# Cosformer attention and a low-rank mixer on one core: tokens dealt five and four to the two halves of the partitions, and another order for batch 0

## The chip, the cores and the metric

The kernel runs on one core of one Trainium2 chip. The metric is device time in microseconds for one execution, lower is better. Each version is timed in several executions; one more is taken by the hardware profiler, and its trace is what the tables and lines here come from.

## The reference, cut to what matters

There are 8 batches of 576 tokens, 8 heads of 64 columns, all in float32. Attention is linear: q and k go through a ReLU and are weighted with a cosine and a sine of the token's position, and softmax is replaced by a division by a sum.

```python
theta = np.pi / 2.0 * pos / S
def phi(x, c, s):
    r = np.maximum(x, 0.0)
    return np.concatenate([r * c, r * s], axis=-1)
kv  = einsum('bhsf,bhsd->bhfd', phi(k), v)          # 128 x 64 for each head
num = einsum('bhsf,bhfd->bhsd', phi(q), kv)
den = einsum('bhsf,bhf->bhs', phi(q), sum_s phi(k)) + 1e-6
x   = num / den                                     # 576 x 512 for each batch
u   = x + (x.T @ U @ V).T                           # mixing of tokens, rank 32
out = u + relu(u @ w_ch1) @ w_ch2                   # 512 -> 2048 -> 512
```

The weights are U (576 x 32), V (32 x 576), w_ch1 (512 x 2048) and w_ch2 (2048 x 512).

## The kernel before, in words

**Tokens on partitions.** 576 tokens are four and a half times 128. Batch b's first 512 tokens are loaded so that partition p holds tokens 4p to 4p+3 (`load_main`, L74): 128 partitions, 8 heads, rows of 1024 bytes. Column group c (0 to 3) of a staging tile is then a tile of 128 tokens. The last 64 tokens form the tail, c = 4, in a tile of its own (`load_tail`, L80: rows of 256 bytes), in the lower 64 partitions for even batches and the upper 64 for odd ones (`tail`, L49), so that two batches' tails fill one tile of 128 tokens. Everything that works with tokens follows this layout: the position weights (iota, L117 and L122), the loads of U (L134, L138), the order of V's columns (`spread_v`, L191) and the stores (L556 for the tails, L560 for the rest: token group c is 128 rows of 2048 bytes, four tokens apart).

**The steps for one batch.** q and k are multiplied on VectorE and ScalarE (`prep`, L228 and L226), v is cast (`v_prep`, `v_block`, L103 and L105). `kv_unit` (L260) gives kv and the denominators' vector for four heads. q is transposed, in batches 0 and 1 on TensorE (`qtr_unit`, L277), later by DMA (`qtr_dma`, L290 and L295). Then come x (`x_unit`, or `den_unit`, L319, and `xh_unit`, L336 and L340, in batch 0), A = x.T U (`A_unit`, L379 and L385), and u = x + V A, both as it is (`u_unit`, L399 and L402) and transposed (`uTd_open`, L438, and `uTd_mm`, L452, in batches 0 and 1; by DMA after that, L422 and L428). The two large products are `g1_main` and `g1_tail` (L487, L507; ScalarE applies the ReLU, L496) and `g2_part` (L540), which adds u on VectorE (L550) and stores.

**What sets the order.** The schedule is written out by hand: each engine runs its instructions in program order. Batches go in pairs; a list of slots has the pair's large products (first batch's g1, second's g1, the tails' g1, then nine blocks of g2), and a table PLAN puts the attention of later batches between them. The head of the program, up to the first g1, has only batch 0's chain: `chain_head`, `chain_mid` and `chain_end` (L645 to L685). It takes four heads at a time; the first four heads' kv, denominators and x run before v of the other four has been cast. It is filled with matmuls on zeros (`keep_warm`, L171: 18, 2 and 13 of them, and seven in `warm0`), whose results nobody reads.

**Queues.** Loads and DMA transposes are issued by SyncE (SP); w_ch1 (`w1_load`, L91) and w_ch2 (`w2_load`, L97) are issued by GpSimd (POOL), which casts them on the way to bf16. The last pair's stores go through SP, the very last part through ScalarE, all others through POOL. POOL's queue in the head: a copy of one column of k's tail (`mark`, L703), which holds back what follows till that has landed, w1's first two quarters, the casts of U and V (`cast_uv`), w1's other two, and a second mark on k of batch 1 (L719), behind which w2 is issued. U and V themselves are the last of SP's loads for batch 0.

**Buffers.** PSUM has eight banks: tags g (3), o (2), T (1) and X (one of two banks). The stores' tile o_sb has four buffers. Each staging tile has one.

Of the kernel before, what the change touches and what calls it, by code (L numbers as in the profile page):

```python
# [13 lines left out]
ALU = mybir.AluOpType  # L14
# [3 lines left out]
def kernel(  # L18
# [29 lines left out]

    def tail(b):  # L49
        lo = TS * (b % 2)  # L50
        return slice(lo, lo + TS)
# [8 lines left out]
    kst, vst, qst, kt, vt, qt = {}, {}, {}, {}, {}, {}  # L60

    def alloc_k(b):
        kst[b] = pool.tile([P, H, 4, D], FP32, tag="kst", bufs=1, name="kst")
        kt[b] = pool.tile([P, H, D], FP32, tag="kt", bufs=1, name="kt")

    def alloc_v(b):
        vst[b] = pool.tile([P, H, 4, D], FP32, tag="vst", bufs=1, name="vst")
        vt[b] = pool.tile([P, H, D], FP32, tag="vt", bufs=1, name="vt")

    def alloc_q(b):  # L70
        qst[b] = pool.tile([P, H, 4, D], FP32, tag="qst", bufs=1, name="qst")
        qt[b] = pool.tile([P, H, D], FP32, tag="qt", bufs=1, name="qt")

    def load_main(dst, src, b, h0=0, h1=H, eng=None):  # L74
        (eng or nc.sync).dma_start(  # L75
            out=dst[:, h0:h1, :, :].rearrange("p h c d -> p h (c d)"),
            in_=src[b, h0:h1, 0:512, :].rearrange("h (p c) d -> p h (c d)", c=4),
        )

    def load_tail(dst, src, b, eng=None):  # L80
        (eng or nc.sync).dma_start(  # L81
            out=dst[tail(b), :, :],
            in_=src[b, :, 512:S, :].rearrange("h s d -> s h d"),
        )
# [16 lines left out]
    def cast(eng, o, i):  # L101
# [10 lines left out]

    alloc_k(0)
    alloc_q(0)
    alloc_v(0)
    iota = const.tile([P, 5], FP32)
    nc.gpsimd.iota(  # L117
        out=iota[:, 0:4], pattern=[[1, 4]], base=0, channel_multiplier=4,
        allow_small_or_imprecise_dtypes=True,
    )  # L120
    for lo in (0, TS):
        nc.gpsimd.iota(  # L122
            out=iota[lo : lo + TS, 4:5], pattern=[[1, 1]], base=512, channel_multiplier=1,
            allow_small_or_imprecise_dtypes=True,
        )
    load_main(qst[0], q, 0)
    load_tail(qt[0], q, 0)
    load_main(kst[0], k, 0)
    load_tail(kt[0], k, 0)
    load_tail(vt[0], v, 0)  # L130
    load_main(vst[0], v, 0, 0, 4)
    load_main(vst[0], v, 0, 4, 8)
    nc.sync.dma_start(out=stV, in_=moe_V)
    nc.sync.dma_start(  # L134
        out=stU[:, 0:4, :], in_=moe_U[0:512, :].rearrange("(p c) r -> p c r", c=4)
    )
    for lo in (0, TS):
        nc.sync.dma_start(out=stU[lo : lo + TS, 4, :], in_=moe_U[512:S, :])  # L138
# [7 lines left out]
    nc.scalar.activation(out=sinw, in_=iota, func=AF.Sin, bias=0.0, scale=scale_ang)  # L146
    nc.scalar.activation(out=cosw, in_=iota, func=AF.Sin, bias=halfpi, scale=-scale_ang)
# [14 lines left out]
    for i in range(2):  # L162
        V_.memset(v_ext[i][:, 4, :, :], 0.0)
        V_.memset(v_ext[i][:, 0:4, :, D:E], 1.0)
        V_.memset(v_ext[i][tail(i), 4, :, D:E], 1.0)
# [10 lines left out]
    V_.memset(U_bf, 0.0)  # L176
    mark = const.tile([TS, 1], FP32)
# [7 lines left out]
    def cast_uv():  # L185
        cast(G_, V_nat, stV)
        cast(G_, U_bf[:, 0:4, :], stU[:, 0:4, :])
        for i in range(2):
            cast(G_, U_bf[tail(i), 4 + i, :], stU[tail(i), 4, :])

    def spread_v(eng):  # L191
# [7 lines left out]
        cast(eng, V_bf, v_ps[:, 0, :].rearrange("r (p c) -> r c p", c=4))  # L199
# [6 lines left out]
    def v_prep(b, h0=0, h1=H, cs=range(5), engs=None):  # L206
        vx = v_ext[b % 2]
        for n, c in enumerate(cs):
            eng = engs[n] if engs else G_
            if eng is None:  # L210
                continue
            if c < 4:
                cast(eng, vx[:, c, h0:h1, 0:D], vst[b][:, h0:h1, c, :])
            else:
                cast(eng, vx[tail(b), 4, h0:h1, 0:D], vt[b][tail(b), h0:h1, :])

    def v_block(b, h0, h1, c0, c1, eng):
# [3 lines left out]
            vst[b][:, h0:h1, c0:c1, :],  # L221
# [10 lines left out]
    def prep(dst, src, b, c, engs, h0, h1):  # L232
        rows = slice(0, P) if c < 4 else tail(b)
# [6 lines left out]
    def k_prep(b, c, engs, h0=0, h1=H):  # L240
        if b not in k_p:
            k_p[b] = pool.tile([P, 4, H, 2 * D], BF16, tag="k_p", bufs=1, name="k_p")
        src = kst[b][:, h0:h1, c, :] if c < 4 else kt[b][:, h0:h1, :]
        prep(k_p[b][:, c] if c < 4 else k_tl, src, b, c, engs, h0, h1)

    def q_prep(b, c, engs, h0=0, h1=H):
        if b not in q_p:
            q_p[b] = pool.tile([P, 4, H, 2 * D], BF16, tag="q_p", bufs=1, name="q_p")
        src = qst[b][:, h0:h1, c, :] if c < 4 else qt[b][:, h0:h1, :]
# [23 lines left out]
    def qtr_unit(b, c, h0=0, h1=H, eng=None, tag="T", bufs=1):  # L273
# [10 lines left out]
        else:  # L284
            cast(eng or V_, q_tlT[:, h0:h1, tail(b)], t_ps[:, h0:h1, tail(b)])

    def qtr_dma(b, c0, c1):
# [6 lines left out]
        else:  # L294
            nc.sync.dma_start_transpose(  # L295
                out=q_tlT[:, :, tail(b)],
                in_=q_tl[tail(b), :, :].rearrange("p h f -> p (h f)"),
# [223 lines left out]
    def g2_part(pr, cc, part):  # L521
# [32 lines left out]
        if cc == 4:  # L554
            for i in range(2):
                eng.dma_start(  # L556
                    out=out[2 * pr + i, 512:S, :], in_=o_sb[i * TS : i * TS + TS, :]
                )
        else:
            eng.dma_start(  # L560
                out=out[b, 0:512, cols].rearrange("(p c) n -> p c n", c=4)[:, c, :],
# [4 lines left out]
    def loads(b, eng):  # L566
        def kk():
            alloc_k(b)
            load_tail(kt[b], k, b, eng)
            load_main(kst[b], k, b, eng=eng)  # L570

        def vv():
            alloc_v(b)
            load_tail(vt[b], v, b, eng)
            load_main(vst[b], v, b, eng=eng)

        def qq():
            alloc_q(b)
            load_tail(qt[b], q, b, eng)
            load_main(qst[b], q, b, eng=eng)  # L580

        return qq, kk, vv
# [21 lines left out]
    def attention_plan(b):  # L604
# [32 lines left out]
        for at, t in zip(lo, loads(b + 1, nc.sync) if lo else ()):  # L637
# [7 lines left out]
    def chain_head(b, fill, xt, engs):  # L645
        v_prep(b, 0, 4, (4,), (engs[0],))
        v_block(b, 0, 4, 0, 3, V_)
        v_block(b, 0, 4, 3, 4, engs[0])
        kv_unit(b, 0, "T", 1)
        fill(0)  # L650
        rec0 = den_unit(b, 0, 4, "X", 1)
        v_prep(b, 4, 8, (4,), (A_,))
        v_block(b, 4, 8, 0, 4, A_)
        fill(1)
        for n, c in enumerate(ORD):
            xh_unit(b, c, 0, 4, rec0, *xt[n])
            if n == 1:
                fill(2)
            if n == 3:
                kv_unit(b, 1, "T", 1, A_)  # L660

    def chain_mid(b, fill, xt, dt):
        fill(3)
        m = 3
        rec1 = den_unit(b, 4, 8, *dt)
        for n, c in enumerate(ORD[:m]):
            xh_unit(b, c, 4, 8, rec1, *xt[n])
        u01 = ps.tile([P, 2, 512], FP32, tag="X", bufs=1, name="u01")
        uTd_open(b, 0, None, None, u01[:, 0, :].rearrange("p (c t) -> p c t", c=4))
        uTd_open(b, 1, None, None, u01[:, 1, :].rearrange("p (c t) -> p c t", c=4))  # L670
        a0 = A_unit(b, "T", 1, A_, 0, 256)
        fill(4)
        uTd_mm(b, 0)
        uTd_mm(b, 1)
        uTd_evac(b, 0, A_)
        uTd_evac(b, 1, A_)
        for n, c in enumerate(ORD[m:]):
            xh_unit(b, c, 4, 8, rec1, *xt[m + n])
        fill(5)
        return a0  # L680

    def chain_end(b, a0):
        A_unit(b, "T", 1, V_, 256, 512, a0)
        uTd_open(b, 2, "o", 2)
        uTd_open(b, 3, "o", 2)  # L685

    def warm0(n):
        m = (2, 1, 0, 1, 1, 2)[n]
        if m:
            keep_warm(m, *(O2 if n == 0 else G3))  # L690

    keep_warm(18, "X", 1)
# [142 lines left out]
```

## Time and profile before

| what | us |
|---|---|
| median of 3 runs | 313.55 (313.11 to 314.17) |
| the profiled execution, its device time | 313.45 |
| its span, first to last instruction | 311.7 |
| TensorE busy with matmuls | 303.7 (97%) |
| VectorE, ScalarE, GpSimd busy | 153.4, 137.5, 46.2 |
| first g1 matmul (L487) starts | 22.98 |
| first g2 matmul (L540) starts, after a wait of 1.04 for w_ch2 | 41.75 |
| last store issued | 308.65 |
| DMA moved | 53.21 MB in 88987 packets, 171 GB/s |

The span is counted from the first instruction; all times of a line are in it. Between the span and the device time lie 1.8 us in which nothing of the program runs. PE is TensorE (PEld its weight loads), DVE VectorE, ACT ScalarE, POOL GpSimd, SP SyncE. L540 is line 540 of the kernel before. In a line of the timeline the first number is the start, the second the duration, both in microseconds, `x4` says that four equal instructions are merged into the line, and the bracket behind has the idle time of the engine ahead of it and what ended that. `DMA_DIRECT2D` is the issue of a transfer, not the transfer; q behind an engine's name is its sequencer.

### The profile page before, as it was taken

To read this page: it belongs to the slowest core of one execution; us is meant where nothing else is said; L and a number is where in the kernel's file an instruction comes from. 1 tells how busy PE (TensorE), PEld (TensorE's weight loads), DVE (VectorE), ACT (ScalarE), POOL (GpSimd) and SP (SyncE) were. 2 spreads that over 40 slices of the span, in tenths; PEclk is the share of its full clock that TensorE was granted. 3 is DMA by queue.
4 is the path that set the end of the run, shared out by engine and by line. 5 is a ranking of instruction groups with operands and counts; after the bars stand their busy time and mean duration, and the time that the engine had idled before them with its cause. 6 is when DMAs were issued, how large, how long until landed. Compare 5 with 4: busy or idle time off the path is not lost.

```text
span 311.7 us, 5648 instructions
## 1 busy us (share of the span) xinstructions
PE 303.7 (97%) x2314; PEld 157.6 (51%) x2314; DVE 153.4 (49%) x340; ACT 137.5 (44%) x229; POOL 46.2 (15%) x85
## 2 busy tenths in 40 slices
PE   7899989999999999999999999999999999999995
PEld 2566445445654444574455444484455444474443
DVE  5868835695878575046426584046426520002111
ACT  3846640265740366669400366669400366640000
POOL 2230300250031007003321400002320100000000
PEclk9999999999999999999999999999999999999999
DMA  7999999989996989992899589922871150001131
GB/s 215 281 244 228 254 183 257 325 200 247 273 178 131 265 200 208 234 306 60 187 226 306 209 103 211 304 76 53 180 157 69 67 86 0 0 2 67 67 103 67
DMA packets 88987, 53.21 MB, mean 171 GB/s; under 512 B 57122, under 2 KB 86178, under 8 KB 88962
## 3 DMA queue, kind: packets, MB, share of 16 engines
q1 hardware_dynamic: 82386, 41.52, 57.2%
q0 software_dynamic: 6432, 11.27, 15.1%
q8 instruction: 18, 0.29, 0.4%
q10 hardware_dynamic: 144, 0.07, 0.1%
q14 instruction: 7, 0.06, 0.0%
HBM read 36.86 MB, written 9.44 MB: 149 GB/s over the span
## 4 chain that ended last, share of the span: by engine, by line
PE 86%; issue 6%; DMA 4%; SPq 2%; POOL 1%; DVE 0%; POOLq 0%
PE o_ps L540 40%; PE g_ps L487 31%; PE gt_ps L507 5%; PE kv_ps L260 3%; PE x_ps L354 3%; DMA vst<-in_v_dram 2%; PE va_ps L399 2%; DMA w_bf<-in_moe_w_ch_dram 2%; SPq L81 1%; PE a_ps L379 1%; POOL w_bf L91 0%; PE va_ps L402 0%; SPq L75 0%; POOL U_bf L105 0%; PE d_ps L319 0%
## 5 line engine op out<-in xcount | busy, mean ns | idle before, releaser
L496 ACT ACTIVATE hid<-g_ps 128x512 bf16<-128x512 f32 x128 | 76.2, 597 | 105.5 <-PE g_ps L487 105.5
L540 PE MATMUL o_ps<-w_bf,hid 128*128 128x512 bf16 (+2 forms) x528 | 120.0, 372 | 1.0 <-DMA w_bf<-in_moe_w_ch_dram 1.0
L487 PE MATMUL g_ps<-uT,w_bf 128*128 128x512 bf16 x512 | 117.8, 379 | 0.1
L487 PEld LDWEIGHTS <-w_bf 128*128 128x128 bf16 x512 | 48.8, 98 | 58.0 <-issue 2.0
L540 PEld LDWEIGHTS <-hid 128*128 128x128 bf16 x528 | 48.2, 98 | 52.0 <-DMA w_bf<-in_moe_w_ch_dram 1.5
L550 DVE TENSOR_TENSOR o_sb<-u_bf,o_ps 128x512 f32<-128x512 bf16 (+2 forms) x33 | 22.0, 668 | 56.3 <-PE o_ps L540 56.2
L560 POOL DMA_DIRECT2D out_dram<-o_sb x24 | 13.2, 550 | 129.5 <-DVE o_sb L550 67.7
L406 DVE TENSOR_TENSOR u_bf<-x_bf,va_ps 128x512 bf16<-128x512 bf16 x32 | 21.9, 686 | 10.4 <-PE va_ps L399 10.4
L105 DVE CAST kv<-kv_ps 128x260 bf16<-128x260 f32 x15 | 6.4, 429 | 38.1 <-PE kv_ps L260 38.1
L364 DVE TENSOR_TENSOR x_bf<-x_ps,rec 128x512 bf16<-128x512 f32 x28 | 19.4, 691 | 1.0
L311 DVE TENSOR_SCALAR rec<-x_ps 128x8 f32<-128x8 f32 (+1 forms) x35 | 5.8, 165 | 22.8 <-PE x_ps L354 22.3
L507 PE MATMUL gt_ps<-uT_tl,w_bf 128*128 128x128 bf16 x256 | 15.9, 219 | 0.0
L507 PEld LDWEIGHTS <-w_bf 128*128 128x128 bf16 x256 | 14.7, 98 | 0.9
L540 PE MATMUL o_ps<-w_bf,hid_tl 128*128 128x512 bf16 x64 | 14.8, 379 | 0.0
L105 POOL CAST v_ext<-vst 128x512 bf16<-128x512 f32 x22 | 13.7, 653 | 3.6 <-DMA vst<-in_v_dram 3.4
L354 PEld LDWEIGHTS <-q_pT 128*128 128x128 bf16 x224 | 10.7, 98 | 6.4 <-DVE x_bf L364 0.4
L174 PE MATMUL w_ps<-zero 128*128 128x512 bf16 x40 | 11.6, 422 | 1.8 <-DVE halfpi L142 1.2
L226 ACT ACTIVATE k_p<-kst,sinw 128x512 bf16<-128x512 f32 x19 | 13.3, 708 | 0.0
L260 PEld LDWEIGHTS <-k_p 128*128 128x128 bf16 x256 | 11.2, 97 | 3.9 <-ACT v_ext L103 0.7
L228 DVE TENSOR_SCALAR q_p<-qst,cosw 128x512 bf16<-128x512 f32 x24 | 12.0, 513 | 2.1 <-DMA qst<-in_q_dram 2.0
L514 ACT ACTIVATE hid_tl<-gt_ps 128x512 bf16<-128x512 f32 x16 | 9.6, 597 | 6.6 <-PE gt_ps L507 6.6
L260 PE MATMUL kv_ps<-v_ext,k_p 128*128 128x65 bf16 x256 | 11.8, 193 | 0.4 <-DVE v_ext L105 0.4
(104 smaller groups left out, 234.2 us busy)
## 6 DMA issues: line engine op xcount, KB each, us to landing
qst<-in_q_dram SPq DMA_DIRECT2D x8, 1024.0 KB, 7.6
kst<-in_k_dram SPq DMA_DIRECT2D x8, 1024.0 KB, 10.3
vst<-in_v_dram SPq DMA_DIRECT2D x7, 1024.0 KB, 10.0
out_dram<-o_sb POOLq DMA_DIRECT2D x24, 256.0 KB, 3.7
w_bf<-in_moe_w_ch_dram POOLq DMA_DIRECT2D x8, 512.0 KB, 11.6
out_dram<-o_sb SPq DMA_DIRECT2D x7, 256.0 KB, 2.3
qt<-in_q_dram SPq DMA_DIRECT2D x8, 128.0 KB, 4.2
kt<-in_k_dram SPq DMA_DIRECT2D x8, 128.0 KB, 7.8
```

What stands on the lines that cost most here:

```text
L105: eng.tensor_copy(out=o, in_=i)
L226: nc.scalar.activation(out=o, in_=i, func=AF.Relu, bias=0.0, scale=w)
L260: nc.tensor.matmul(out=acc[:, i, :], lhsT=k_p[b][:, c, h, :] if c < 4 else k_tl[:, h, :], rhs=vx[:, c, h, :], start=(c == 0), stop=(c == 4),)
L354: nc.tensor.matmul(out=acc[:, g, i * E : i * E + E], lhsT=qT_of(b, c, h), rhs=kv_sb[b][:, h, :], start=True, stop=True,)
L364: nc.vector.tensor_tensor(out=x_of(b, c, rows).rearrange("p (g i d) -> p g i d", g=2, d=D), in0=view[:, :, :, 0:D], in1=rec[rows].unsqueez ...
L406: nc.vector.tensor_tensor(out=u_bf[b][:, c, :] if c < 4 else u_tl[b // 2], in0=x_of(b, c), in1=va, op=ALU.add,)
L487: nc.tensor.matmul(out=g_ps.rearrange("p (c t) -> p c t", c=4), lhsT=w1_bf[:, d, j * P : j * P + P], rhs=uT[b][:, :, d, :], start=(d == 0) ...
L496: nc.scalar.activation(out=hid[b][:, j, :], in_=g_ps, func=AF.Relu, bias=0.0, scale=1.0)
L507: nc.tensor.matmul(out=g_ps[:, jj, :], lhsT=w1_bf[:, d, j * P : j * P + P], rhs=uT_tl[pr][:, d, :], start=(d == 0), stop=(d == 3),)
L540: nc.tensor.matmul(out=o[:, cols], lhsT=lhs[:, j, c * P : c * P + P], rhs=w2_bf[:, j, cols], start=(j == 0), stop=(j == NJ - 1),)
L550: nc.vector.tensor_tensor(out=o_sb[:, cols], in0=u[:, cols], in1=o[:, cols], op=ALU.add)
L560: eng.dma_start(out=out[b, 0:512, cols].rearrange("(p c) n -> p c n", c=4)[:, c, :], in_=o_sb[:, cols],)
```

## The change

Token m*9+k goes to another place. Of each nine tokens in a row, the first five go to partition m (of 0 to 63) and the other four to partition 64 + m. There are no tail loads: a tensor's load is one transfer to the lower 64 partitions (rows of 1280 bytes) and one to the upper 64 (1024). Column group c (0 to 3) then holds tokens 9m+c and 9m+5+c; c = 4, which is the tail, holds tokens 9m+4, in the lower half, for every batch. The transposes put an odd batch's tail into the upper half of the shared tile, as before.

```diff
-            in_=src[b, h0:h1, 0:512, :].rearrange("h (p c) d -> p h (c d)", c=4),
...
-            in_=src[b, :, 512:S, :].rearrange("h s d -> s h d"),
...
+    def load(dst, src, b, h0=0, h1=H, engs=(nc.sync, nc.sync)):
+        nines = src[b].rearrange("h (m k) d -> m h (k d)", k=9)[:, h0:h1]
+        for eng, rows, k0, n in zip(engs, (LO, HI), (0, 5), (5, 4)):
+            eng.dma_start(
+                out=dst[rows, h0:h1, 0:n, :].rearrange("m h c d -> m h (c d)"),
+                in_=nines[:, :, k0 * D : k0 * D + n * D],
+            )
```

The stores follow. The order of dimensions on the DRAM side of the second is block (two of them), row (64), column:

```diff
                 eng.dma_start(
-                    out=out[2 * pr + i, 512:S, :], in_=o_sb[i * TS : i * TS + TS, :]
+                    out=out[2 * pr + i].rearrange("(m k) n -> m k n", k=9)[:, 4, :],
+                    in_=o_sb[i * TS : i * TS + TS, :],
                 )
         else:
             eng.dma_start(
-                out=out[b, 0:512, cols].rearrange("(p c) n -> p c n", c=4)[:, c, :],
+                out=out[b].rearrange("(m k) n -> k m n", k=9)[c : c + 6 : 5, :, cols],
                 in_=o_sb[:, cols],
             )
```

U and V are loaded by POOL as its first four transfers, ahead of all its other DMAs, instead of last by SP. V's cast is three strided copies instead of one flat one. POOL's order in the head becomes: U and V, their casts, a mark on the lower half of v's first four heads, all four quarters of w1, a mark on the same place of batch 1's v, w2:

```diff
-    G_.tensor_copy(out=mark, in_=kt[0][0:TS, 0, 0:1])
-    w1_load(0)
-    w1_load(1)
     cast_uv()
-    w1_load(2)
-    w1_load(3)
-    chain_head(0, warm0, (O2, O2, G3, G3, O2), (A_,))
...
+    G_.tensor_copy(out=mark, in_=vst[0:TS, 3, 4, 0:1])
+    for n in range(4):
+        w1_load(n)
+    first_chain(0)
+    load(qst, q, 1)
+    load(kst, k, 1)
+    load(vst, v, 1, 0, 4)
+    load(vst, v, 1, 4, 8)
+    G_.tensor_copy(out=mark, in_=vst[0:TS, 3, 4, 0:1])
     for n in range(4):
         w2_load(n)
```

Batch 0's chain becomes one function. Both halves of v are cast first; the two kv and the two denominators stand side by side in banks of their own, and the parts of x get their PSUM tiles one after the other. There are 13 + 5 + 13 fills and none inside the chain (`warm(...)` is defined and not called):

```diff
+    def first_chain(b):
+        v_block(b, 0, 4, 0, 3, V_)
+        v_block(b, 0, 4, 3, 4, A_)
+        v_prep(b, 0, 4, (4,), (A_,))
+        v_block(b, 4, 8, 0, 3, V_)
+        v_block(b, 4, 8, 3, 4, A_)
+        v_prep(b, 4, 8, (4,), (A_,))
+        kv_unit(b, 0, *T1)
+        kv_unit(b, 1, *O2, A_)
...
+        den_mm(b, 0, 4, d[0])
+        den_mm(b, 4, 8, d[1])
+        x0 = [xh_mm(b, c, 0, *t) for c, t in zip(ORD, (G3, G3, G3, O2, O2))]
+        recip(rec[0], d[0])
+        V_.tensor_scalar(out=rec[1], in0=d[1], scalar1=1e-6, scalar2=None, op0=ALU.add)
+        xh_norm(b, ORD[0], 0, rec[0], x0[0])
+        V_.reciprocal(out=rec[1], in_=rec[1])
+        for n in range(1, 5):
+            xh_norm(b, ORD[n], 0, rec[0], x0[n])
+        x1 = [xh_mm(b, c, 4, *t) for c, t in zip(ORD, (T1, G3))]
+        spread_v(A_)
+        x1 += [xh_mm(b, c, 4, *t) for c, t in zip(ORD[2:], (G3, G3, O2))]
+        for n in range(5):
+            xh_norm(b, ORD[n], 4, rec[1], x1[n])
...
+        a_mm(b, a_ps, 0, 256, range(5))
+        cast(A_, A_of(b)[:, 0:256], a_ps[:, 0:256])
...
+        for i in range(2):
+            open_mm(b, i, t[i], range(4))
+        uTd_mm(b, 0)
+        uTd_evac(b, 0, A_)
+        uTd_mm(b, 1)
+        uTd_evac(b, 1, V_)
+        a_mm(b, a_ps, 256, 512, range(5))
+        cast(A_, A_of(b)[:, 256:512], a_ps[:, 256:512])
+        open_mm(b, 3, t[3], range(4))
+        open_mm(b, 2, t[2], range(4))
```

The transposes of batch 0's q keep their order on TensorE but all five come ahead of the five copies out of PSUM in the program. From the first g1 on, the instructions of the engines and their order are those of before, apart from the layout of what they load and store.

## The prediction

> **What bounds the kernel now.** I read the stages first: busy time of each engine in seven stretches (start:end, length, then busy us and instructions of PE, PEld, DVE, ACT, POOL, the clock, the DMA share, GB/s).
>
> ```profile
> 7.60:14.60 7.00, 5.97 (x56) 3.76 (x57) 6.38 (x15) 6.97 (x12) 2.22 (x3) 1.00 1.16 287
> 14.60:23.00 8.40, 8.07 (x164) 5.67 (x164) 5.21 (x16) 3.75 (x8) 2.69 (x6) 1.00 1.17 247
> ...
> 40.70:308.30 267.60, 266.52 (x1969) 137.18 (x1968) 122.70 (x265) 112.45 (x187) 36.37 (x58) 1.00 0.68 161
> 308.30:311.70 3.40, 0.00 (x0) 0.00 (x0) 0.29 (x1) 0.00 (x0) 0.00 (x0) 0.95 0.23 77
> ```
>
> From 40.70 to 308.30 PE is busy 266.52 of 267.60 us; what the change does off PE there costs nothing until it makes PE wait. Only the head (to 41 us) and the 3.4 us behind PE's last matmul are open. In 7.60 to 14.60 ACT is busy 6.97 of 7.00: in the head's middle the preparation of q and k sets the pace, not the loads.
>
> Then the waits (us in total, times, longest), for the head:
>
> ```profile
> PE o_ps L540 <- DMA w_bf<-in_moe_w_ch_dram: 1.0, 1, 1.0
> ...
> DVE v_ext L105 <- DMA vst<-in_v_dram: 0.8, 2, 0.4
> ```
>
> PE's one DMA wait is 1.04 us at 41.75, for w2's first quarter. Faster v loads have little to give: before the first v cast DVE waits 0.41 us.
>
> Last the timeline of the last pair's stores, L560 (L556 the tail's). These decide.
>
> ```profile
> 281.38 10.69 SPq L560 DMA_DIRECT2D out_dram<-o_sb  x4
> ...
> 295.20 1.20 SPq L556 DMA_DIRECT2D out_dram<-o_sb  x2
> ...
> 298.65 9.70 SPq L560 DMA_DIRECT2D out_dram<-o_sb  x4
> ...
> 308.65 0.37 ACTq L560 DMA_DIRECT2D out_dram<-o_sb  x1
> ```
>
> One 256 KB store is due every 3.45 us. The DMA view of a stretch around one of them (299 to 301) shows its 128 rows and 16 completions as packets:
>
> ```profile
> DMA packets 144, 0.26 MB, mean 131 GB/s; under 512 B 16, under 2 KB 16, under 8 KB 144
> ...
> out_dram<-o_sb SPq DMA_DIRECT2D x1, 256.0 KB, 2.3
> ```
>
> In the packet records a 2048-byte row takes 86 ns (median; least 81), the 128 rows go from 299.49 to 300.32, and 16 engines at 8 rows x 86 ns are 0.69 us. So the stores now use a fifth of their time and only the last is seen: issue 308.65, last row 309.90, landed 310.43, end of span 311.66.
>
> **Part 1, the output stores (L560): the large term.** Before, the DRAM side of a store is 128 rows at one step. After, tokens c and c+5 of each nine go out together, so it is two blocks of 64 rows; the instruction listing has 2x64x512 where 128x512 stood. The bytes and row lengths are unchanged. What can change is over how many of the 16 engines the rows are spread, and no row here has a leading dimension of 2. Nearest rows: transfers with 32, 64 or 128 leading rows, and the 1x1 gate (L740). Queue q1 has 2097 four-byte completion packets: 63 other transfers at 16 and 34 transposes at 32 make 2096, which leaves one for the gate. A leading size of 1 ran on one engine, of 32 and more on 16; 2 lies nearest to 1, so I take two engines. Bounds: 16 engines as now, cost 0; two engines, 64 rows each, 64 x 81 to 86 ns = 5.2 to 5.5 us a store, against one due every 3.45.
>
> The Trainium skill speaks against this change: "DMA: Bandwidth & Descriptors", section "Why a DMA increments its semaphore by 16 and not by 1", says that a transfer runs on the largest number up to 16 that divides the slowest dimension of both sides. By it 2 and 128 give 2, on SP's queue always the lowest-numbered two, while GpSimd's queue moves on through the engines; the sum would be the one below. The gate's single completion agrees; no run here shows a 2.
>
> With the same two engines each time (my choice: one shape on one queue), the backlog at 5.5 us runs, in before's times: first row 282.24; four stores end 304.24; the tail store, still 64 leading rows, adds 8 rows, 0.69: 304.93; three stores 321.43; the 384-column part 64 x 67 ns = 4.29: 325.72; the 128-column part, 64 x 27 ns = 1.73: 327.45. With the 0.53 to landing and 1.23 to the end of the span, 329.2 against 311.66: **+17.6**; at 5.2 us a store **+14.8**. I take +16.2. DVE's adds wait for no buffer beyond about 1 us: o_sb has four, and the store four back has just landed each time.
>
> **Part 2, the same stores in mid-run, on POOL's queue.** There a store is 64 packets of 4096 bytes at 171 ns: 0.7 us over 16 engines, 5.5 over two. Stores come 4 to 5 us apart, their buffers last. What can hurt is a load or transpose that must pass those two engines. The tightest row is batch 2's second transpose of u (L422): issued 98.40, landed 101.94, read by PE at 102.89, 0.95 us of slack, with stores issued at 95.50 and 100.30. Behind one whole store it would be up to 4 us late; shared, about 1.8. The other transposes of u have 1.8 us and more, and fall mostly where no store is under way. I take **+0.8**, bounds 0 and 4.
>
> **Part 3, the loads and the head.** Per tensor 1024 rows of 1024 B and 512 of 256 B (46 and 18 ns alone: 3.52 us over 16 engines) become 512 of 1280 and 512 of 1024 B; by the slope of those rows 1280 B is 55 ns, together 3.24 us. Between 9.4 and 11.4, when 256 B rows prevail, the DMA view has 191 GB/s against 282 in 1.7 to 6.0, so crowded loads gain more. But ACT hides it: q lands at 6.73 now and, both halves and the few U and V bytes ahead, at about 6.9. V's three strided casts on POOL (0.66 for one flat cast now) lie idle-side, ahead of w1's issue: at most 0.7 late there.
>
> Then by rows: ACT's k work ends 13.65; four v casts (0.42, 0.40, 0.42, 0.40) to 15.3, beside two of DVE (0.56 each). kv0 starts 14.5 (14.60 now), kv1 15.35 (17.05 now). The first denominator stands behind kv1 on PE: 16.0 (15.88 now), the second 16.65. DVE then has 0.46 + 0.18 + 0.28 of reciprocals and ten multiplications (two of 0.42, eight of 0.35): from 16.7, with a 0.2 wait, to 21.4 (22.24 now). Behind it A, its cast on ACT and two evacuations put PE's first g matmul at about 22.5 (22.98 now): **-0.45**. Bounds -1.5 and +1.5. The bad end is w1's first quarter, which landed at 22.80, with PE reading it at 22.93: its gate moves from k's tail (landed 11.85) to v's first half (about 11.7 to 12), so it stays level, with no slack.
>
> The fills go from 40 to 31, and two gaps open on PE of about 2 us each (5.5 to 7.7 and 12.7 to 14.5; the largest now is 0.9). If the clock fell in one, the price is that of the cold start: 18 fills take 5.52 us where 18 x 0.216 is 3.9, so 1.6 us. The granted clock is 1.00 in every full stretch and no row shows a 2 us gap, so I take 0 and keep 1.6. (The skill's "TensorE: Matmul & The Clock Gate", Part 1, lets the clock fall after an idle window of about 3.4 us; by it these gaps cost nothing.)
>
> **Part 4, w2's wait.** It goes if w2's first quarter comes no later than PE (40.71 - 0.45 = 40.26). The 3072 rows of 256 B of batches 0 and 1 took 3.5 us (18 ns) to 6.0 us (31 ns, beside w1); the wider rows take back 1.8. Against that, w2's gate moves from k of batch 1 to the first half of its v, half a MB later, 1.4 us at the 355 KB that the packet records have in the head's full microseconds. Landing: 41.70 less 0.3 to 2.8. In the middle the wait is gone: **-1.04**, bounds -1.04 and +0.1.
>
> **Sum.** +16.2 + 0.8 - 0.45 - 1.04 = +15.5. The profiled execution took 313.45 us (span 311.66 and 1.8 around it), against a median of 313.55: 313.45 + 15.5 = **329.0**.
>
> **Rivals.**
> - *The stores still spread over 16 engines.* Parts 3 and 4 stay: 313.45 - 1.5 = 312.0, not slower. For it: bytes and rows are the same, and the SBUF side still has 128 rows. Against: the gate's single completion. It decides from about 8 engines upwards, where a store takes 1.4 us.
> - *Two engines, but others for each store.* Only the last is late: 308.85 + 4.29 + 1.76 = 314.9 against 311.66, +3.25; with parts 2 to 4 316.0. It needs an assignment that moves; no row speaks to it.
> - *Two engines, and PE also starves in mid-run:* the transposes of u late by 4 us in two of the three pairs, +7: 336.
> - *POOL's stores all on the same two engines:* 24 x 5.5 = 132 us beside 0.7 x 190 us of their usual work is some 60 us too much: about 390.
>
> **How the numbers follow.** Forecast 0.70, 16 engines 0.12, moving pairs 0.09, starving 0.07, overrun 0.02. The range, 315.5 to 336.5, takes in forecast, moving pairs and starving, and leaves out 0.14 and the tails. Within 0.3% (0.9 us, about what a measurement of this kernel can tell from no change): the 16-engine case at 312.0 is faster unless the head fails it: faster 0.09, same 0.04, slower 0.87.
>
> **What would show it.** Right: PE ends near 308, the last stores land 10 to 18 us later, SP's stores take far more than 2.3 us to landing and each later one more; the DMA share is near an eighth in the last 45 us. Wrong: a store still lands in 2.3 us, and the span ends 3.4 us after PE. Head: first g matmul at 22.5, no wait for w2. Clock: a granted clock below 1.00 between 5 and 25 us. What would most upset the forecast is a row at 45 ns on an engine that has little company.

## The result, and the profile after

The changed kernel takes **382.51 us** (median of five runs, 378.77 to 384.47) against 313.55 for the kernel before; the ratio is 1.2183 (95% interval 1.2099 to 1.2267). The direction was forecast, the size was not: +69.0 us where the prediction has +15.5 and a range that ends at 336.5. The profiled execution took 381.92 us, with a span of 380.1. An execution that fell into a slower state is left out of every ratio here, and of the time given for the loads in halves.

| point in the span, us | before | after | later by |
|---|---|---|---|
| first g1 matmul | 22.98 | 29.29 | 6.3 (head) |
| last store issued | 308.65 | 363.54 | 54.9, so 48.6 in the middle |
| end of the span | 311.66 | 380.12 | 68.5, so 13.6 in the tail |

The last store issued is 2.6 us later than it need be because its add waits for a buffer that an earlier store still holds (`DVE o_sb L564 <- DMA out_dram<-o_sb: 2.6, 1, 2.6`). That share of the 48.6 belongs to the tail, so some 46.0 are the middle's and 16.2 the tail's.

First the stretches of the kernel after, in the columns of the first fence of the prediction: two of the head, the middle from the first g2 matmul to the last matmul, the tail.

```profile
7.60:14.60 7.00, 4.75 (x45) 3.77 (x46) 4.71 (x9) 4.34 (x6) 2.98 (x6) 0.76 1.11 225
14.60:29.30 14.70, 10.76 (x169) 7.32 (x170) 9.19 (x25) 6.62 (x15) 3.55 (x5) 0.88 1.14 238
46.60:360.90 314.30, 279.29 (x1945) 141.16 (x1967) 121.47 (x265) 111.67 (x187) 51.67 (x58) 0.94 0.93 134
360.90:380.10 19.20, 0.00 (x0) 0.00 (x0) 0.29 (x1) 0.00 (x0) 0.00 (x0) 0.59 0.12 46
```

In the middle PE is idle for 35.0 us (314.30 less 279.29; 1.1 before), and the same matmuls take 12.8 us longer (279.29 against 266.52; 24 of their records are missing in the trace after) while the granted clock is 0.94 where it was 1.00. The DMA engines are busy 0.93 of the time instead of 0.68, and move 134 GB/s instead of 161: they are held, not used. In the head ACT, busy 6.97 of 7.00 before, is busy 4.34: now it waits for loads.

The waits of the kernel after (us in total, times, longest); the two of PE are in the middle, that of ACT in the head:

```profile
POOL v_ext L92 <- DMA vst<-in_v_dram: 63.1, 7, 27.1
...
PE x_ps L368 <- DMA q_pT<-q_p: 16.0, 4, 4.5
...
PE g_ps L501 <- DMA uT<-u_bf: 11.2, 2, 8.9
...
ACT q_p L227 <- DMA qst<-in_q_dram: 6.2, 1, 6.2
```

27.2 us of PE's idle time are waits for DMA transposes. The wait for w2 ahead of the first g2 is gone, as forecast. On the list of DMA issues (KB each where it is given, median us to landing), GpSimd's stores and the transposes of q and u, first before, then after:

```profile
out_dram<-o_sb POOLq DMA_DIRECT2D x24, 256.0 KB, 3.7
...
q_pT<-q_p SPq DMA_TRANSPOSE x12, 5.4
uT<-u_bf SPq DMA_TRANSPOSE x12, 3.5
```

```profile
out_dram<-o_sb POOLq DMA_DIRECT2D x24, 256.0 KB, 13.9
...
q_pT<-q_p SPq DMA_TRANSPOSE x12, 17.6
uT<-u_bf SPq DMA_TRANSPOSE x12, 10.5
```

The last pair's stores in the timeline of SP's sequencer:

```profile
333.97 10.87 SPq L575 DMA_DIRECT2D out_dram<-o_sb  x4
347.78 1.80 SPq L570 DMA_DIRECT2D out_dram<-o_sb  x2
351.23 14.19 SPq L575 DMA_DIRECT2D out_dram<-o_sb  x4
```

Between 335 and 374.5 the 2048-byte rows of these stores come at some 24 a us with two under way at a time, 84 ns each (the tail's two stores apart, which are not in blocks): two engines, as forecast, and two completion packets for each of SP's stores where there were 16.

### The profile page after: what moved, and what is told of

Its sections match the earlier page's. It is cut to its first block, busy times and chain, and to the rows that moved or that the text cites. A ratio compares the mean times of both kernels' runs of the same rounds, so it can differ in the third digit from the quotient of the medians.

```text
span 380.1 us, 5616 instructions
## 1 busy us (share of the span) xinstructions
PE 317.4 (83%) x2279; PEld 163.1 (43%) x2305; DVE 152.5 (40%) x341; ACT 136.1 (36%) x231; POOL 65.3 (17%) x91
## 4 chain that ended last, share of the span: by engine, by line
PE 58%; DMA 27%; SPq 7%; issue 1%; DVE 1%; POOL 1%; DVEq 0%; POOLq 0%
PE g_ps L501 26%; PE o_ps L554 22%; DMA vst<-in_v_dram 10%; DMA uT<-u_bf 5%; DMA q_pT<-q_p 5%; SPq L304 4%; DMA w_bf<-in_moe_w_ch_dram 3%; SPq L68 3%; DMA out_dram<-o_sb 3%; PE gt_ps L521 3%; PE kv_ps L261 2%; PE x_ps L368 2%; PE va_ps L413 2%; DVE o_sb L564 1%; PE t_ps L278 1%
## 5 line engine op out<-in xcount | busy, mean ns | idle before, releaser
L501 PE MATMUL g_ps<-uT,w_bf 128*128 128x512 bf16 x512 | 119.5, 383 | 12.7 <-DMA uT<-u_bf 11.2
L554 PE MATMUL o_ps<-w_bf,hid 128*128 128x512 bf16 (+2 forms) x509 | 125.9, 390 | 1.5 <-issue 0.7
L554 PEld LDWEIGHTS <-hid 128*128 128x128 bf16 x528 | 50.2, 101 | 55.6 <-issue 9.3
L564 DVE TENSOR_TENSOR o_sb<-u_bf,o_ps 128x512 f32<-128x512 bf16 (+2 forms) x33 | 22.1, 669 | 59.6 <-PE o_ps L554 56.0
L575 POOL DMA_DIRECT2D out_dram<-o_sb x24 | 19.5, 814 | 137.4 <-DVE o_sb L564 114.0
L92 POOL CAST v_ext<-vst 128x512 bf16<-128x512 f32 (+1 forms) x28 | 28.9, 1062 | 63.3 <-DMA vst<-in_v_dram 63.1
L368 PE MATMUL x_ps<-kv,q_pT 128*128 128x65 bf16 x224 | 13.7, 210 | 20.4 <-DMA q_pT<-q_p 16.0
L420 DVE TENSOR_TENSOR u_bf<-x_bf,va_ps 128x512 bf16<-128x512 bf16 x32 | 22.0, 686 | 11.7 <-PE va_ps L413 10.8
L368 PEld LDWEIGHTS <-q_pT 128*128 128x128 bf16 x224 | 12.1, 109 | 29.8 <-DMA q_pT<-q_p 17.9
L554 PE MATMUL o_ps<-w_bf,hid_tl 128*128 128x512 bf16 x61 | 15.9, 408 | 0.2
## 6 DMA issues: line engine op xcount, KB each, us to landing
kst<-in_k_dram SPq DMA_DIRECT2D x8, 512.0 KB, 12.7
w_bf<-in_moe_w_ch_dram POOLq DMA_DIRECT2D x8, 512.0 KB, 12.9
```

Source lines behind the costliest of these rows:

```text
L92: eng.tensor_copy(out=o, in_=i)
L368: nc.tensor.matmul(out=acc[:, g, i * E : i * E + E], lhsT=qT_of(b, c, h), rhs=kv_sb[b][:, h, :], start=True, stop=True,)
L420: nc.vector.tensor_tensor(out=u_bf[b][:, c, :] if c < 4 else u_tl[b // 2], in0=x_of(b, c), in1=va, op=ALU.add,)
L501: nc.tensor.matmul(out=g_ps.rearrange("p (c t) -> p c t", c=4), lhsT=w1_bf[:, d, j * P : j * P + P], rhs=uT[b][:, :, d, :], start=(d == 0) ...
L554: nc.tensor.matmul(out=o[:, cols], lhsT=lhs[:, j, c * P : c * P + P], rhs=w2_bf[:, j, cols], start=(j == 0), stop=(j == NJ - 1),)
L564: nc.vector.tensor_tensor(out=o_sb[:, cols], in0=u[:, cols], in1=o[:, cols], op=ALU.add)
```

## The experiments

Each edit is shown in part: lines left out are marked `...`, and comments in the edits are notes to the reader. Each run's ratio is to the kernel before timed beside it (313.62 to 314.25 us).

### Stores that use 16 engines, with everything else of the change

```diff
-                out=out[b].rearrange("(m k) n -> k m n", k=9)[c : c + 6 : 5, :, cols],
...
+            for rows, k0 in ((LO, c), (HI, c + 5)):   # one transfer for each half
+                eng.dma_start(
+                    out=out[b].rearrange("(m k) n -> m k n", k=9)[:, k0, cols],
+                    in_=o_sb[rows, cols],
```

> The changed kernel, each store of a token group issued as two transfers, one for each half of the partitions, 64 rows each; loads and chain as changed. Theory S (stores whose leading dimension is 2 run on two engines, and this is what made both the middle and the end of the run late): the last store lands about 3 us after its issue instead of 16.5, PE no longer waits for transposes in the middle, and only the head's 6.3 us stay: 318 to 322 us. Theory L (loads into one half of the partitions at about 225 KB/us instead of 355 are what made the middle late): the end is repaired (13.5 us) but not the middle: 350 to 370 us.

321.18 us, ratio 1.0265 (1.0203 to 1.0327): 61.3 of the 69.0 us go with this one change. PE's waits for transposes are gone; the head's are left:

```profile
PE t_ps L290 <- ACT q_p L227: 4.1, 1, 4.1
PE g_ps L501 <- DMA w_bf<-in_moe_w_ch_dram: 1.6, 1, 1.6
```

The first g1 starts at 29.21, 6.2 late, and 7.1 us over the kernel before timed beside it (314.06) remain.

### Two, four and eight blocks, on the kernel before

The kernel before gets stores with a leading dimension of 2, 4 or 8 on the DRAM side (k = 8, 16, 32; rows are stored in another order):

```diff
-                out=out[b, 0:512, cols].rearrange("(p c) n -> p c n", c=4)[:, c, :],
+                out=out[b, 0:512, cols].rearrange("(m k) n -> k m n", k=8)[c::4, :, :],
```

> The kernel before with one edit: each store of a token group goes to two blocks of 64 rows (leading dimension 2 on the DRAM side), so that output rows 0 to 511 of a batch are permuted. Loads, layout and chain are those of before. Theory S: two engines for each store, so the end is late by 13 to 17 us and the middle by some 40: 355 to 370 us. Theory L: only the end is late: 326 to 331 us. If the count of engines is not set by the leading dimension: 313.5 us.

> As e2_two_blocks, but four blocks of 32 rows (leading dimension 4; output rows permuted). If the leading dimension sets the count of engines, a store has 32 rows on each of four engines, 32 x 84 ns = 2.7 us, less than the 3.45 us between two stores, so no backlog grows: the end is late by about 2 us and the middle by little, 315 to 322 us. If instead the order of rows in DRAM is what is slow, it is as late as e2_two_blocks.

> The kernel before with stores of eight blocks of 16 rows in every pair (rows stored in another order). Two blocks gave 379, four 332. Theory S (as many engines as the leading dimension has): eight engines carry 16 rows each, some 1.4 us at 85 ns for SyncE's, 8 completions a store, about 64 padding packets by the count of 32 for each idle engine in GpSimd's stores where two blocks had 448 and four 384 at most; nothing piles up, and a residue of 0 to 5 us is left: 314 to 319. Rival (a placement that is not the leading dimension, so that eight is no better than four): 328 or more.

| blocks | us | ratio (95%) | completions of one SP store | 8-byte packets of one POOL store |
|---|---|---|---|---|
| 2 | 379.32 | 1.2067 (1.2011 to 1.2123) | 2 | 448 |
| 4 | 332.42 | 1.0584 (1.0531 to 1.0636) | 4 | 192 |
| 8 | 319.54 | 1.0159 (1.0122 to 1.0196) | 8 | 64 |

So a store runs on as many engines as its leading dimension has, and two blocks alone cost 65.3 us on the kernel before, more than the 41 to 56 that I had expected of them. The loss falls much faster than the engines' number rises (65, 18, 5). Four blocks cost more than I had expected: at 2.7 us a store (32 rows of 84 ns) on four engines none should wait for the last, and yet GpSimd's took 7.8 us to land and the transposes came late.

### Tail and middle apart

Two blocks in the last pair alone (stores of SP), and in the other three alone (stores of POOL):

```diff
+                out=out[b, 0:512, cols].rearrange("(m k) n -> k m n", k=8)[c::4, :, :]
+                if pr == NPAIR - 1     # the other kernel: if pr < NPAIR - 1
+                else out[b, 0:512, cols].rearrange("(p c) n -> p c n", c=4)[:, c, :],
...
```

> The kernel before with two-block stores (a leading dimension of two, rows of batches 6 and 7 stored in another order) in the last pair alone, whose stores SyncE issues; the other three pairs' stores as before. This is the tail that the prediction priced at 16.2 (14.8 to 17.6), without the middle. Theory M (the tail as priced, and the middle lost by transposes and loads held back beside GpSimd's two-block stores): first matmul to last as before (end of TensorE near 310.6), the last store 13 to 17 us after it, time 326.5 to 331, so that the middle's share of the 379 of two-block stores everywhere is 48 to 53. Rival (the two-block stores collide only with each other, and the middle's loss hangs on the tail's queue too): under 322 or over 335.

> The kernel before with two-block stores in pairs 0 to 2 alone (GpSimd's stores; rows stored in another order), the last pair's as before. Theory: middle and tail add up, so that this costs what two blocks everywhere cost (65.3) less the last pair's (16.0): 363 +- 3, the last store 3 to 4 us from the end. Rival (the last pair's stores have their share in the middle's loss, or the tail's price is less when the clock has fallen): under 357 or over 368.

The last pair alone: 329.57 us, 1.0513 (1.0491 to 1.0535), +16.0, with the middle as before and the loss behind PE's end:

```profile
40.70:308.30 267.60, 266.46 (x1968) 137.23 (x1968) 122.59 (x265) 112.36 (x186) 36.23 (x58) 1.00 0.68 159
308.40:327.50 19.10, 0.00 (x0) 0.00 (x0) 0.29 (x1) 0.00 (x0) 0.00 (x0) 0.60 0.12 46
```

The other three pairs alone: 362.12 us, 1.1539 (1.1484 to 1.1594), +47.9; the last store is issued 3.0 us from the end, as before. 16.0 and 47.9 make 63.9 of the 65.3. PE's waits in the second kernel:

```profile
PE x_ps L354 <- DMA q_pT<-q_p: 20.1, 4, 7.9
PE g_ps L487 <- DMA uT<-u_bf: 8.4, 2, 7.2
```

### Bytes or placement: narrow two-block stores

```diff
+                out=out[b, 0:512, 0:64].rearrange("(m k) n -> k m n", k=8)[c::4, :, :]
+                if pr < NPAIR - 1
...
```

> The kernel before with two-block stores in pairs 0 to 2, each cut to columns 0 to 63 (256 of a row's 2048 bytes; the other columns of these rows are not written); the last pair stores as before. As many rows and the same placement on two engines as in the two-block kernel, with an eighth of the bytes. Theory B (the middle is lost to the bytes that two engines carry, which hold the transposes' packets behind them): 64 rows a carrying engine at 18 to 30 ns, where a 256-byte packet took 18 in the kernel before, are 1.2 to 1.9 us of a store due every 3.45, so transposes and loads run as before and the time is 313 to 317. Rival N (the padding packets or the placement itself, however few the bytes): the middle's loss of 48 to 50 stays in good part, over 335.

314.32 us, ratio 1.0007 (0.9990 to 1.0023). Two engines cost nothing when they carry little: here a store is eight packets of 4096 bytes instead of 64. So placement alone is not the cost. But the packets that GpSimd's stores post for the idle engines (last column of the table) fall with the bytes, from 448 to 56 a store, so this run does not part the time for which two engines are held from those packets. Against the packets stands the changed kernel's trace: its 10752 of eight bytes take 171 us summed over 16 engines, 11 us an engine in the whole run, and between 115 and 118 us, where the transposes are slow, only 33 of them go and take 3 us of the 16 engines' 48.

### The change without its later loads

```diff
-                for dst, src in ((qst, q), (kst, k), (vst, v))]
+                for dst, src in ((qst, q), (kst, k), (vst, v)) if b < 3]
```

> The changed kernel with the loads of batches 3 to 7 left out (their attention works on batch 2's q, k and v again); stores on two engines as in the change, DMA transposes as before, so that in the middle only stores and transposes are left on the DMA engines. Theory T (the stores hold the transposes directly): TensorE still waits for q_pT and uT by more than half of the 31 us that it waited in the changed kernel, and the time is 350 to 375. Rival C (the loads are what takes too long beside the stores, and the transposes only stand behind them on SyncE's queue): these waits fall under 8 us, and the time is 330 to 343, tail and head alone.

372.94 us, ratio 1.1870 (1.1818 to 1.1923). The loads of five batches are gone and the waits stay:

```profile
PE x_ps L368 <- DMA q_pT<-q_p: 19.8, 4, 8.1
PE g_ps L501 <- DMA uT<-u_bf: 9.1, 1, 9.1
```

The stores hold the transposes directly; what the loads add is about 10 us (382.51 less 372.94).

### Loads in halves

The kernel before, with each main load as two transfers, partitions 0 to 63 and 64 to 127:

```diff
+        for rows in (slice(0, TS), slice(TS, P)):
+            (eng or nc.sync).dma_start(
+                out=dst[rows, h0:h1, :, :].rearrange("p h c d -> p h (c d)"),
+                in_=main[rows],
...
```

> The kernel before with each main load of q, k and v issued as two transfers, one for each half of the partitions (same rows of 1024 bytes, same places); stores and chain of before. Theory L: a row takes about 80 ns instead of 46 to 48, batch 0's q lands at about 8.5 instead of 6.7 and v's first half at about 15.5 instead of 14.0, and the head and perhaps the middle are late: 317 to 330 us. Theory S: the loads are hidden as before and what they cost is 0 to 3 us: 313.5 to 316.5. If both halves overlap on the engines anyway, rows stay at 46 to 48 ns.

326.3 us (two executions), 1.0389 (1.0327 to 1.0451). In the head its 1024-byte rows take 80 ns where whole loads took 46 to 48, and the tail of batch 1's q is late:

```profile
DVE q_tl L230 <- DMA qt<-in_q_dram: 6.4, 1, 6.4
```

Then the change with split stores, and batch 0's two halves from two queues:

```diff
-    load(qst, q, 0)
+    BOTH = (nc.sync, nc.scalar)
+    load(qst, q, 0, engs=BOTH)        # k and v likewise
```

> The changed kernel with the split stores (321.2 us), and in it batch 0's loads for partitions 64-127 issued by ScalarE's queue beside those for 0-63 on SyncE's, instead of after them on the same queue. Theory P (each half of the partitions takes only some 200 KB/us, both together 355, so halves must travel together): batch 0's rows fall from 80 and 103 ns back towards 46 to 60, q is consumed near 7, the second half of v is in by 16, w1's loads are issued near 14 instead of 16.4, first g1 24 to 26 instead of 29.2, time 316 to 318.5. Rival Q (a 64-partition transfer has slow packets whatever runs beside it): rows stay at 80 and 103 ns, first g1 at 29 +- 0.7, time 320.5 to 322. Either may be 0.5 to 1.5 worse because ScalarE now spends 0.6 to 1.2 us on each of four issues ahead of its first activations.

319.11 us, 1.0185 (1.0158 to 1.0213), 2.1 better than the split stores by the medians; the intervals of the two ratios still touch. The stretch 8 to 15, first of the split stores, then of this kernel (the last number is GB/s):

```profile
8.00:15.00 7.00, 5.05 (x37) 4.03 (x38) 4.60 (x8) 3.73 (x6) 3.05 (x6) 0.51 1.10 225
```

```profile
8.00:15.00 7.00, 5.22 (x38) 4.12 (x39) 4.52 (x8) 3.89 (x6) 2.67 (x6) 0.54 1.09 328
```

One half at a time moves 225 GB/s, both beside each other 328; in 10 to 15 us the rows fall from 83 and 98 ns (1024 and 1280 bytes) to 53 and 62. Theory P holds for the rates, though q itself came no sooner (8.90): at first the two queues were served one after the other, and the first g1 (26.40) and the time stay just outside its ranges.

### What sets the head

w1 gated on k instead of v; 26 fills ahead of q's transposes instead of 13; both; and 12 more fills, eight of them inside the chain:

```diff
+    G_.tensor_copy(out=mark, in_=kst[0:TS, 0, 0, 0:1])   # w1's gate (split stores)
+    w1_load(0)
+    w1_load(1)
     cast_uv()
...
-    keep_warm(13, "X", 1)                                # fills (two queues)
+    keep_warm(26, "X", 1)
```

> The changed kernel with the split stores (321.2 us), with w1's loads gated on k's lower half (landed 12.4) as in the kernel before, two of them ahead of the casts of U and V, instead of on v (16.3). Theory G (the late gate of w1 is a cost by itself): w1's first load is issued near 12.7 and lands near 25.5 instead of 29.2; the first g1 then waits for the chain, at about 27.8 (it waited 1.4 us for w1 alone), time about 319.8. Rival L (the slow halves of the loads set the head; w1 sent earlier takes its share from v): v's last half lands 1 to 3 us later than 19.9, the first g1 is at 28.5 to 31, time 320.5 to 323.

> The changed kernel with split stores and two queues for batch 0 (319.1 us), with 26 instead of 13 matmuls on zeros ahead of q's transposes, so that TensorE doesn't sit idle for 3.7 us before them. Theory W (w1's arrival at 26.0 sets the first g1 at 26.4, whatever the clock): granted clock 1.00 from 8 to 15, q's transposes done by 13.5 instead of 15.7, the first g1 still at 26.0 to 26.5, time 318.6 to 319.3. Rival K (the fallen clock is what the head pays for): first g1 under 25.5, time under 318.

> The run with 26 fills, and w1 gated on k's lower half as well, as in the run of w1's gate alone (which by itself was 1.8 us worse than the split stores). Theory W: with the chain no longer held by the clock, the earlier w1 (issued near 13, landed near 23 to 24) now counts: first g1 at 24 to 25.3, time 317 to 318.5. Rival L (w1 sent earlier takes the engines' time from v and from batch 1's loads, which are late in its place): first g1 at 25.5 or more or a wait behind it, time 319 to 321.

> The run with 26 fills (323.8 us, granted clock 0.50 from 19.5 to 29.7, in the middle of batch 0's chain, which has no fills of its own), with 12 more: four ahead of the chain and eight inside it (after both kv units, after both denominators, before A's second half is needed). Theory K (the changed chain on late loads pays by the fallen clock, because its fills are gone): granted clock 1.00 from 15 to 30, first g1 at 25.0 to 27.2 (w1's first quarter landed at 26.0 to 27.2), time 317.5 to 320, at least 3.5 better than 323.8. Rival (the 4.7 us between the run with 26 fills and the one with 13 come from something else, as loads landing later): the clock holds and the time stays over 321.5; or the clock falls all the same, and the question stays open.

| kernel | us | ratio (95%) | w1's first quarter issued, landed | first g1 |
|---|---|---|---|---|
| split stores | 321.18 | 1.0265 (1.0203 to 1.0327) | 16.43, 29.16 | 29.21 |
| and w1's gate on k | 323.02 | 1.0288 (1.0261 to 1.0315) | 12.54, 25.52 | 27.11 |
| split stores, two queues | 319.11 | 1.0185 (1.0158 to 1.0213) | 15.62, 26.00 | 26.40 |
| and 26 fills | 323.82 | 1.0299 (1.0255 to 1.0344) | 15.60, 27.15 | 27.42 |
| and w1's gate on k | 321.03 | 1.0215 (1.0151 to 1.0279) | 13.77, 25.73 | 27.33 |
| 26 fills and 12 more | 325.28 | 1.0342 (1.0275 to 1.0409) | 16.82, 29.66 | 29.70 |

None of the fills helped, and theory K's forecast of the time fails: with all of them the granted clock is 1.00 to 28.5, the chain is done at 26.2, and PE then waits for w1.

```profile
25.83 0.39 PE L704 MATMUL uT_ps<-ident,x_bf 128*128 128x128 bf16 x4
29.70 1.04 PE L502 MATMUL g_ps<-uT,w_bf 128*128 128x512 bf16 x2 [3.49 <-DMA w_bf<-in_moe_w_ch_dram]
```

Where w1 is gated on v, W was right that its arrival sets the first g1, and wrong that it stands still; with the gate on k, w1 was there 1.6 us before the first g1, which the chain then set. With a faster chain, batch 0's k is used up sooner, so SP issues batch 1's k at 16.68 (26 fills) and 16.43 (12 more) instead of 18.93, and its packets go beside w1's or ahead of them. An earlier gate brings w1 sooner and batch 1's loads later (with the gate on k, k of batch 1 landed at 38.5 instead of 35.8, and the first g2 waited 1.2 us for w2). The head's DMA is full (1.09 to 1.17 of the mean engine's time; packets overlap), and who goes first only decides who is late. That the order of issues is the cause is read from the traces; no run isolates it, and of the steps in this table only that from 13 to 26 fills is clear of the ratios' intervals. Some 3 us of the 4.7 between 26 fills and 13 lie behind the first g1, spread, and stay open.

### The other parts by themselves, on the kernel before

The new order of batch 0 alone (`first_chain` with the transposes of q in separate banks); U and V first in POOL's queue alone; w2's first quarter behind a mark on k's tail instead of k:

```diff
-    G_.tensor_copy(out=mark, in_=kst[1][0:TS, 7, 3, 0:1])
+    G_.tensor_copy(out=mark, in_=kt[1][tail(1), 0, 0:1])
+    w2_load(0)
+    G_.tensor_copy(out=mark, in_=kst[1][0:TS, 7, 3, 0:1])
```

> The kernel before with the third part's order of batch 0 alone (the transposes of q in separate banks, both kv units together, first_chain), and nothing else: loads, stores, U, V and w1's gate as before. In the kernel before w1's first load lands at 22.80 and the first g1 begins at 22.98, so if w1 sets that point the new order buys nothing: 313.2 to 314.2, first g1 22.9 to 23.2. Rival (the chain itself was late, or the new order is worse for want of fillers between its steps): first g1 moves by over 0.5 us either way with w1 landed before it, and the time with it: 312.5 to 313.1, or 314.3 to 316.

> The kernel before with U's and V's four loads moved from the end of SyncE's queue to the front of GpSimd's, and nothing else. With the run of the new order of batch 0 alone (no difference) this leaves only layout and stores of the change. Theory: their 147 KB travel beside q's, so q lands 0.3 to 0.6 us later than 6.73, and the point that counts, w1's arrival at 22.80, moves by less than 0.4 us: 313.2 to 314.2. Rival (SyncE's queue, freed of four issues, sends batch 1's loads 1 to 2 us earlier, ahead of w1's packets): w1 lands 0.5 us or more later, 314.2 to 315.5.

> The kernel before with the first quarter of w2 gated on k's tail of batch 1 (landed 29.0) instead of k's main load (36.0); the other three quarters as before. The third part's term for w2 alone, without the change's loads. Theory: the first quarter is issued near 29.3 instead of 36.2, lands before 40, and the wait of 1.04 us of the first o_ps at 41.75 goes: 312.5 to 313.0. Rival (its transfer comes between k's and w1's, and they are late instead): k of batch 1 lands 2 us later than 36.0, or w1's last quarter after 36, g1 or batch 1's preparation waits, and the time is 313.6 to 315.

All three change nothing: 1.0002 (0.9989 to 1.0015), 0.9995 (0.9977 to 1.0014), 1.0000 (0.9986 to 1.0014). With the new order w1 lands at 22.90 and the first g1 starts at 22.99, as before (22.80, 22.98). With U and V first the profiled run had its first g1 at 25.84, though w1 had landed at 22.93 (the chain was late, not w1), and yet ended only 1.6 us later: a late first g1 is not always paid in full. With w2 early the wait of 1.04 at the first g2 is gone and k of batch 1 lands at 37.55 instead of 35.99. No kernel tried beats the kernel before.

## Why the prediction was wrong, step by step

- **Part 1, the tail: right.** Two engines, +16.2 forecast, 16.0 measured for the last pair alone. (By its own steps the lower sum is some +15.0, not +14.8; and the last add's wait for a buffer was 2.6 us, not 1.) The four-byte completion of the gate was a good witness, and the Trainium skill's rule ("DMA: Bandwidth & Descriptors", section "Why a DMA increments its semaphore by 16 and not by 1") holds for 2, 4 and 8, by the completions in the table.
- **Part 2, the same stores in the middle: this step failed.** +0.8, at most 4, forecast; 47.9 measured. The step is "Behind one whole store it would be up to 4 us late; shared, about 1.8", for one transpose with one store under way. The row I had picked was the right one, the second transpose of each of these lines of SP's sequencer, before and after:

```profile
95.82 4.59 SPq L422 DMA_TRANSPOSE uT<-u_bf  x2
```

```profile
108.69 9.28 SPq L436 DMA_TRANSPOSE uT<-u_bf  x2
```

  Batch 2's second transpose of u took 3.54 us from issue to landing; after the change it is issued at 111.27 and PE has it at 124.81, 13.5 later and 8.9 of it idle. But there was not one store: POOL's stores of 5.1 us (32 packets of 159 ns on each of two engines), due every 4 to 5 us, themselves took 12.6 and 12.9 us to land, and from 108.4 on two or three were open all the while. Here is the DMA view of 111 to 124, in 40 slices (busy tenths, then GB/s):

```profile
DMA  3246979992661999991199999999990399999799
GB/s 65 60 104 125 163 132 166 123 79 64 84 61 52 72 82 56 58 67 40 40 82 65 66 54 50 36 167 211 175 24 8 78 286 137 223 231 168 132 213 254
```

  From 115 to 119.5, while PE waits, nearly every slice is full, at 36 to 82 GB/s. Over the whole run the 256-byte packets, mostly the transposes', took 18 ns in the median as before, but 178 at the 95th percentile instead of 40; between 115 and 119 their median was 168, about as long as one packet of a store (159). A transpose's packets are spread over all engines (by its 32 completions, two for each of 16), so it ends with the slowest; I had taken the other 14 engines as free. Three quarters of the 256-byte packets of 115 to 119 took over 100 ns, though, with one or two packets of a store under way at a time: more than the engines that carried the stores was slow, and what ties the others to them no run shows. I had also priced only u's transposes in two pairs: q's (`qtr_dma`) cost PE more, 16.0 against 11.2 us. And where PE sat idle the granted clock fell to 0.50: in or after each of its six gaps of 3.5 us or more in the middle, as from 118.5 to 128.7, and not after the one of 2.4. PE is busy for 26.7 us at that clock, and half of that is about the 12.8 us. The starving rival had the mechanism at 7 us. The rival at 390 came nearer in its number, by luck: it had all of POOL's stores on the same two engines. The records have no engine numbers, but from 122.3 to 126, with two of POOL's stores open, four packets of 4096 bytes are under way most of the time, at 159 ns each as ever, where SP's stores in blocks have two, however many are open. By that count those two stores ran on four engines.
- **Part 3, loads and head: failed.** -0.45 forecast, +6.3 at the first g1. Two steps: "by the slope of those rows 1280 B is 55 ns", where they took about 100 (101 in the median of the run), and "ACT hides it", which turned round: q was there at 9.07 instead of 6.9, and ACT waited 6.2 us for it. The trace of before had the row that I passed over: the tail's store L556 uses 64 partitions, and its 2048-byte rows took 155 ns where 128 partitions had 86. The Trainium skill had it too: "SBUF — State Buffer", section "Door 1: The DMA port swizzle (why `[64,N]` ≈ `[32,N]`)", has partitions 0 to 63 on eight of 16 ports, with some 218 GB/s; the 225 above are near it. The same page, in "Can I just issue two DMAs to hit both halves?", denies that two transfers help (6%); from two queues they gave 328 instead of 225 here, and the measurement decides. The chain's -0.45 was not to be had: w1's arrival set the first g1 already, at 22.80. And its gate was to open at "about 11.7 to 12" with v's first half, which landed at 16.26: w1 was issued at 16.58 instead of 12.23, which is 4.35 of the 6.44 us by which it landed later (29.24); the rest is its packets' way beside slow loads. The bound of +1.5 had room for neither.
- **The clock.** I kept 1.6 for two gaps of 2 us; the first became 3.4 us, as q came late, and the granted clock was 0.50 from 9.3 to 12.7. Kept at 1.00 by the fills, the clock bought nothing in the total.
- **Part 4, w2: the wait went, the gain did not come.** Alone it is worth 0.0 of the 1.04. Batch 1's loads are later in its place (k by 1.56 us); that this is where the gain went is likely, but no run shows it.
- **The sum.** The stores are 61.3 us; split stores leave 7.1 of the change, for the loads by exclusion, as U and V first, the new order and w2's gate each alone change nothing. The range excluded what happened because Part 2's bounds were one transfer's wait, not a queue's.

## What to carry to other kernels

Before costing a transfer, look at the leading dimension of both sides and at the partitions that it spans: with two blocks it used two engines, and with 64 partitions little more than half of the rate (rows of 1024 bytes 80 ns instead of 46 to 48), and in both cases the bytes and row lengths said nothing of it. A transfer on few engines is priced by what crosses those engines, for as long as they are held out of each interval (5.1 us out of 4 to 5 here), not by its own lateness. And a wait that ends with a DMA in a stretch where the DMA engines are full may not be a gain to be had: here, moving one transfer forward moved another back.

## What the runs showed of the hardware

- Loads to half of the partitions begin at full speed: until 4.0 us rows of 1280 bytes took 55 ns (1024: 46), some 300 to 400 KB, and then some 100 to 110 (75 to 90). Why the first go faster no run shows.
- GpSimd's stores on k engines post packets of eight bytes for the others: 14 x 32 for two blocks, 12 x 16 for four, 8 x 8 for eight, as many for each idle engine as a working one has data packets. In the changed kernel their own time is 11 us an engine; no run has two-block stores of full size without them, so what they cost is not known.
- The granted clock also fell without a long gap: with 26 fills it was 0.50 from 19.5 to 29.7, and the largest gap in the 5 us before was 0.86, among short matmuls.
